# Queries loaded and paired outputs stored in 4096-byte pieces per partition

## The chip, the cores and the metric

The kernel runs on one core of a Trainium2 chip. A core has a matrix engine (TensorE, called PE in the profile; its weight loads are shown apart as PEld), a vector engine (VectorE, DVE), an engine for activation functions (ScalarE, ACT), a general engine (GpSimd, POOL), and an engine that mostly issues transfers (SyncE, SP; its queue is SPq). Sixteen DMA engines move data between the device memory and the on-chip memory of 128 partitions. The engines run side by side, each through its own list of instructions in order; semaphores hold one back until another has come far enough.

The metric is the device time of one execution in microseconds (us); lower is better.

## The reference

The kernel computes an attention over spatially reduced keys, then a mixture of eight small adapters of which each token uses the best two. Reduced to what matters (4 batches of 12288 tokens of 128 channels; 768 pooled keys for a batch):

```python
kv_pool = kv.reshape(B, H // 4, 4, W // 4, 4, C).mean(axis=(2, 4))
k = v = kv_pool.reshape(B, -1, C) @ w_sr
a = softmax(q @ k.T / sqrt(C))
x = a @ v                                   # 49152 tokens x 128
logits = x @ w_gate                         # 8 gates; the best 2 are kept
w = softmax(best 2 logits)
out = x + sum over the 2 chosen e of w[e] * ((x @ A[e]) @ B[e])
```

Every token is computed by itself, given the keys and values of its batch. So the order in which tokens are put into partitions does not matter for the result, as long as the outputs are stored where the queries came from.

## The kernel before, in words

**Tiles.** A chunk is 512 tokens: 128 partitions times four tokens (`NS = 4`). There are 96 chunks (`NCH`), 24 to a batch. Two neighbouring chunks, 2i and 2i + 1, form a pair of 1024 tokens (`HROWS`). Queries are loaded by pairs, gates are sent by pairs, outputs are mostly stored by pairs.

**Which token sits where.** `load_q` (L100) reads a pair as `(k p s) c -> p k (s c)`: partition p holds, of each chunk k of the pair, the four neighbouring tokens 4p to 4p + 3. These are 4 x 128 x 4 bytes = 2048 bytes side by side in device memory, once for each of the two chunks, 256 KB apart. Two more places load queries in the same order: L125 loads the first four chunks (`q0`, 1 MB) in one transfer, and `load_half` (L127) the pairs 2 and 3 into buffers that later hold kv rows. The outputs follow: `give` (L510) gathers a pair in one tile `osb` and stores it in one transfer of the same form (L518), `put` (L503) stores the single chunks at the end of the program, 2048 bytes from each partition, 256 KB in one stretch of the device memory.

**Way of a chunk.** The queries of a pair are cast to 16 bits (`cast_q`, POOL, L107) and turned by a DMA transpose (`turn_q`, SPq, L117), so that channels lie across partitions. `scores` (L326, L327) multiplies keys with them on PE, two key tiles of 128 at a time, and takes the exponential on ACT. `weigh` (L338) multiplies the exponentials with the values; `normalise` (L345 to L356) divides by the sum and finds the best gates on DVE. `gate` (POOL, L365 to L369) and a tanh on ACT make the gates of a pair. They are turned by a small DVE transpose, written to device memory (`send_gates`, L425 and L426) and read back, broadcast over the rows of the adapters (`load_gates`, L433, tile `ge`). The output of `normalise` is turned on PE (L405) and copied by DVE (L416), multiplied with A (L440), gated by DVE (L443, which needs `ge`), multiplied with B (L486) and added to x (L500).

**Order.** It is written out by hand. The main loop (L683) runs over the chunks; in one turn it issues the scores of a later chunk, the weighing of the chunk before, and the adapter stages of chunks six to nine turns back (`lag`, L668). In every second turn it also issues the transpose of the queries three pairs ahead, the load of the queries about five pairs ahead, and the transfers of the gates. The kv rows of the next batch are loaded (L87) and summed (POOL, L191 to L196) in turns fixed by `plan` (L276). Nearly every transfer is issued by SPq, one after another, in this order. Only the four small weight loads at the start are issued by ACT.

**Start.** SPq issues the four kv rows of the first key tile, then `q0`, then the eight kv rows of tiles 1 and 2, then four query loads of 512 KB. The first four chunks are turned on PE (L590) and not by DMA. The last six chunks have their own code after the loop (from L749), in which single chunks are stored by `put`.

Of the kernel before, what the change touches and what calls it, by code (L numbers as in the profile page):

```python
# [21 lines left out]
def kernel(  # L22
# [10 lines left out]
    nc = tc.nc  # L33
    P = 128
# [6 lines left out]
    NTOK = 512  # L41
    NS = NTOK // P
# [31 lines left out]
    qflat = q.rearrange("b n c -> (b n) c")  # L74
# [14 lines left out]
    def load_kv(b, t):  # L89
        for d in range(4):  # L90
            load_row(b, t, d)

    GROWS = 2048

    HROWS = GROWS // 2
    q32, q16, qT = {}, {}, {}

    def load_q(i):  # L100
        q32[i] = qpool.tile([P, 2, NS * C], FP32, tag="q32", name="q32", bufs=3)
        nc.sync.dma_start(q32[i], qflat[i * HROWS:(i + 1) * HROWS].rearrange(
            "(k p s) c -> p k (s c)", p=P, s=NS))

    def cast_q(i):
        new_q16(i)
# [13 lines left out]
    q0, q1 = q01[:, 0], q01[:, 1]  # L120
    for t in range(NT):
        load_kv(0, t)
        if t == 0:

            nc.sync.dma_start(q0, qflat[0:GROWS].rearrange("(k p s) c -> p k s c", p=P, s=NS))  # L125

    def load_half(i):  # L127
        q32[i] = q1[:, 2 * i - 4:2 * i - 2].rearrange("p k s c -> p k (s c)")
        nc.sync.dma_start(q32[i], qflat[i * HROWS:(i + 1) * HROWS].rearrange(
            "(k p s) c -> p k (s c)", p=P, s=NS))  # L130

    load_half(2)
    load_q(4)
    load_half(3)
    load_q(5)

    w_in = const.tile([P, P], FP32)
# [359 lines left out]
    def add_rows(c, lo=0, hi=NS, osb=None, bank_=None):  # L497
        osb = half_out() if osb is None else osb
        d = dps[c][:, lo:hi] if bank_ is None else bank_
        nc.vector.tensor_tensor(osb[:, lo:hi], d, xn[c][:, lo:hi, 0:C], op=ALU.add)  # L500
        return osb

    def put(c, osb, lo=0, hi=NS, queue=None):  # L503
        t0 = c * NTOK
        (queue or nc.sync).dma_start(
            out[t0:t0 + NTOK, :].rearrange("(p s) c -> p s c", p=P)[:, lo:hi], osb[:, lo:hi])

    opair = {}

    def give(c):  # L510

        if c % 2 == 0:
            opair[c // 2] = run.tile([P, 2, NS, P], FP32, tag="osb", name="osb", bufs=3)
        o = opair[c // 2]
        add_rows(c, osb=o[:, c % 2])
        if c % 2:
            t0 = (c - 1) * NTOK
            nc.sync.dma_start(  # L518
                out[t0:t0 + 2 * NTOK, :].rearrange("(k p s) c -> p k (s c)", p=P, k=2),
                o.rearrange("p k s c -> p k (s c)"))  # L520

    spare = []

# [159 lines left out]
    for c in range(2, NCH - 1):  # L683
        b, k = divmod(c, CPB)
# [4 lines left out]
        if c % 2 and (c + 11) // 2 < 2 * NQ:  # L689
            load_q((c + 11) // 2)  # L690
# [12 lines left out]
        for x in ups.get(c, ()):  # L703
            up(x, None if x == ups[c][-1] else t_bank())
            give(x)
# [103 lines left out]
    n = NCH - 1  # L809
# [22 lines left out]
    gated_hidden(n - 6)  # L832
    up(n - 7, bank(0))
    put(n - 7, add_rows(n - 7))
    weigh(n - 1, 1)
    tops4(n - 1, top4, y4)
# [33 lines left out]
    turn(high(n), 0, NS, bank(0), xT, n)  # L870
    add(n - 6, o6, nc.gpsimd)
    put(n - 6, o6)
    gate_args(n, 0, NS, nc.gpsimd, top5, arg5, msk5)
    gate_tanh(0, NS, arg5)
    up(n - 3, mtile([P, NTOK], name="d2"))
    gated(n - 1, 0, NS, arg4, h4)
    put(n - 3, add_rows(n - 3))
    up(n - 2)
    o3 = take(n - 2)
# [33 lines left out]
    with tc.If(bad_v != 0):  # L913
# [11 lines left out]
        with tc.For_i(0, B) as b:  # L925
            nc.sync.dma_start(kp, kp_all[bass.ds(b, 1)].rearrange("o p k -> p (o k)"))
            for h in range(2):
                s = slice(h * NKV // 2, (h + 1) * NKV // 2)
# [3 lines left out]
            for h in range(2):  # L932
                v_ps = mtile([P, NJ // 2, C + E], name="gv_ps")
                for g in range(NJ // 2):
                    j = h * NJ // 2 + g
# [3 lines left out]
            with tc.For_i(0, N, P) as t:  # L939
                t0 = b * N + t  # L940
# [19 lines left out]
                for h in range(2):  # L960
                    e_ps = mtile([P, NJ // 2, P], name="ge_ps")
                    for g in range(NJ // 2):
                        j = h * NJ // 2 + g
# [70 lines left out]
```

## Time and profile before

| | |
|---|---|
| median of 3 runs | 376.8 us (375.92 to 378.57) |
| the profiled execution, its time | 375.43 us |
| the profiled execution, its span from first to last instruction | 373.6 us |
| instructions | 10589 |
| DMA packets, bytes | 95594, 101.01 MB |
| read from device memory, written to it | 62.33 MB, 25.90 MB |
| mean granted clock of TensorE | 0.996 |

The span begins with the first instruction and ends with the last; the execution's own time holds some 1.8 us more. In a row of grouped instructions stand the line of the kernel, the engine, the operation, what is written and read, the count, the busy time in all and the mean time of one. In a timeline the first two columns are the start and the length in us, and a bracket gives the idle time before and what ended it. In a list of waits the columns are the time in all, how often, and the longest. Transfers are cut into packets, one for each piece that is contiguous on both sides; the DMA share is the time of the packets over the time of 16 engines, and since packets of one engine can overlap, it can be above 1.

### The profile page before, as it was taken

The page shows a single profiled execution, that of the slowest core. Times are in us where ns is not written, and L with a number is a line of the kernel's source. Part 1 is how long each engine was busy: PE and PEld are TensorE (multiplying, and loading weights), DVE is VectorE, ACT ScalarE, POOL GpSimd, SP SyncE. Part 2 cuts the span into 40 slices and gives each one's busy share as a digit, 9 for nine tenths or more (in the row PEclk, how much of TensorE's full clock was granted, in tenths as well). Part 3 has the DMA queues.
Part 4 walks back from the last instruction along what each step waited for, and adds up shares of the span by engine and source line. Part 5 has one row for each costly group of instructions (what it writes and reads, how often), then busy time and mean ns, then how long its engine had stood idle before and what let it go on. Part 6 is the DMA issues. An engine that isn't in the chain of part 4 may idle for free.

```text
span 373.6 us, 10589 instructions
## 1 busy us (share of the span) xinstructions
PE 356.5 (95%) x3942; PEld 262.8 (70%) x3943; DVE 299.6 (80%) x952; ACT 309.4 (83%) x391; POOL 225.6 (60%) x376
## 2 busy tenths in 40 slices
PE   4789999999999999999999999999999999999983
PEld 2456777777777677777777777777776767667772
DVE  3784558888888788888888888888888898998983
ACT  1579999989889798898898898898888888888862
POOL 1013799988799897755679697755444234232255
PEclk9999999999999999999999999999999999999998
DMA  8998999999999999999999999998789799663325
GB/s 261 413 360 218 316 300 304 298 318 306 286 335 320 308 292 331 226 317 314 304 288 361 303 313 317 253 302 260 227 225 257 206 255 245 184 145 131 130 86 201
DMA packets 95594, 101.01 MB, mean 270 GB/s; under 512 B 58804, under 2 KB 59060, under 8 KB 95540
## 3 DMA queue, kind: packets, MB, share of 16 engines
q1 hardware_dynamic: 94068, 100.11, 94.6%
q8 instruction: 31, 0.51, 0.6%
q10 hardware_dynamic: 1472, 0.20, 0.3%
q14 instruction: 23, 0.19, 0.2%
HBM read 62.33 MB, written 25.90 MB: 236 GB/s over the span
## 4 chain that ended last, share of the span: by engine, by line
PE 83%; DVE 5%; POOL 4%; DMA 3%; ACT 2%; issue 1%; SPq 0%; POOLq 0%; DVEq 0%
PE xps L338 33%; PE sg L326 30%; PE t_ps L405 5%; PE d_ps L486 5%; PE h_ps L440 4%; DMA kvt<-in_kv_dram 2%; DMA ge<-g_h 2%; ACT tt L327 1%; PE v_ps L215 1%; POOL osb L495 1%; DVE xn_all L349 1%; DVE osb L500 1%; DVE ht L443 1%; DVE kvt L191 1%; PE k_ps L240 1%
## 5 line engine op out<-in xcount | busy, mean ns | idle before, releaser
L327 ACT ACTIVATE tt<-sg 128x1024 f16<-128x1024 f32 x288 | 276.9, 1023 | 36.3 <-PE sg L326 35.5
L326 PE MATMUL sg<-qT,kfT 128*128 128x512 f16 x576 | 170.2, 379 | 0.5 <-ACT qT L593 0.3
L338 PEld LDWEIGHTS <-tt 128*128 128x128 f16 x2304 | 146.1, 98 | 28.4 <-DVE xn_all L349 18.1
L338 PE MATMUL xps<-vext,tt 128*128 128x136 f16 x2256 | 164.7, 223 | 0.3 <-DVE xn_all L349 0.2
L500 DVE TENSOR_TENSOR osb<-d_ps,xn_all 128x512 f32<-128x512 f32 x85 | 58.7, 691 | 28.7 <-PE d_ps L486 27.7
L365 POOL TENSOR_TENSOR arg<-xn_all,top 128x64 f32<-128x64 f32 x47 | 14.5, 308 | 99.6 <-DVE top L356 80.2
L349 DVE TENSOR_TENSOR xn_all<-xps,rinv_all 128x540 f32<-128x540 f32 x94 | 67.7, 721 | 3.3
L326 PEld LDWEIGHTS <-kfT 128*128 128x128 f16 x576 | 49.1, 98 | 24.4 <-issue 1.5
L191 POOL TENSOR_TENSOR kvt<-kvt 128x1024 f32<-128x1024 f32 x27 | 63.7, 2361 | 2.1 <-PE t_ps L405 2.0
L107 POOL CAST q<-q 128x1024 f16<-128x1024 f32 x45 | 46.8, 1042 | 24.0 <-DMA q<-in_q_dram 24.0
L443 DVE SCALAR_TENSOR_TENSOR ht<-ge,h_ps 128x512 bf16<-128x512 f16 x87 | 58.5, 673 | 1.4 <-DMA ge<-g_h 1.0
L486 PEld LDWEIGHTS <-ht 128*128 128x128 bf16 x368 | 27.0, 98 | 24.6 <-DVE ht L443 5.7
L356 DVE MAX8 top<-xn_all 128x8 f32<-128x8 f32 x376 | 35.1, 156 | 6.3
L416 DVE COPY xt<-t_ps 128x512 bf16<-128x512 bf16 x92 | 36.8, 400 | 0.0
L405 PE MATMUL t_ps<-id_bf,xn_all 128*128 128x128 bf16 x376 | 36.3, 219 | 0.0
L486 PE MATMUL d_ps<-b_bf,ht 128*128 128x128 bf16 x340 | 32.9, 219 | 0.8 <-DVE ht L443 0.7
L440 PE MATMUL h_ps<-xt,a_bf 128*128 128x512 bf16 x86 | 32.6, 379 | 0.1
L345 DVE RECIPROCAL rinv_all<-xps 128x4 f32<-128x4 f32 x94 | 17.1, 182 | 13.6 <-PE xps L338 12.2
L405 PEld LDWEIGHTS <-xn_all 128*128 128x128 bf16 x376 | 25.9, 98 | 0.3
L368 POOL TENSOR_SCALAR msk<-msk 128x64 f32<-128x64 f32 x47 | 20.2, 429 | 4.1
L369 POOL TENSOR_TENSOR arg<-arg,msk 128x64 f32<-128x64 f32 x47 | 15.1, 321 | 3.9
L367 POOL TENSOR_TENSOR arg<-arg,msk 128x64 f32<-128x64 f32 x47 | 15.1, 320 | 3.7
(150 smaller groups left out, 221.0 us busy)
## 6 DMA issues: line engine op xcount, KB each, us to landing
kvt<-in_kv_dram SPq DMA_DIRECT2D x48, 512.0 KB
q<-in_q_dram SPq DMA_DIRECT2D x46, 512.0 KB
out_dram<-osb SPq DMA_DIRECT2D x44, 512.0 KB
ge<-g_h SPq DMA_DIRECT2D x45, 256.0 KB
out_dram<-osb SPq DMA_DIRECT2D x8, 256.0 KB
q<-in_q_dram SPq DMA_DIRECT2D x1, 1024.0 KB
qT<-q SPq DMA_TRANSPOSE x46
g_h<-g_sb SPq DMA_DIRECT2D x45, 16.0 KB
```

The source lines that it names most:

```text
L107: nc.gpsimd.tensor_copy(q16[i], q32[i].rearrange("p k n -> p (k n)"))
L191: eng.tensor_tensor(v[:, 0], v[:, 0], v[:, d], op=ALU.add)
L326: mm(sg[:, k], kfT[b][:, j * P:(j + 1) * P], qc, start=True, stop=True)
L327: nc.scalar.activation(tt[c][:, 2 * r:2 * r + 2], sg, AF.Exp, bias=0.0, scale=scale)
L338: mm(o, tt[c][:, j, s * P:(s + 1) * P], vext[b][:, j, 0:VW], start=(j == 0 and s % 2 == 0), stop=(j == NJ - 1 and s % 2 == 1), skip_group_ ...
L349: nc.vector.tensor_tensor(xn[c][:, :, 0:C + G].rearrange("p (b s) v -> p b s v", b=2), xv[:, :, :, 0:C + G], ri.rearrange("p (b s) -> p b ...
L405: mm(columns(t_ps, c, s), src[:, s], id_bf, is_transpose=True, start=(s == 0), stop=(s == NS - 1), skip_group_check=True)
L416: nc.vector.tensor_copy(to, t_ps)
L440: mm(h_ps, a_bf, xT[c], start=True, stop=True)
L443: nc.vector.scalar_tensor_tensor(hgT[c].rearrange("p (k a) t -> p k (a t)", k=2), gE[c // 2][:, h:h + NS // 2].rearrange("p a t k -> p k ( ...
L486: mm(dps[c][:, s], columns(hgT[c], c, s), b_bf, start=(s == 0 and fresh), stop=(s == NS - 1), skip_group_check=True)
L500: nc.vector.tensor_tensor(osb[:, lo:hi], d, xn[c][:, lo:hi, 0:C], op=ALU.add)
```

## The change

Partition p holds eight neighbouring tokens of a pair, 8p to 8p + 7: the first four count as its tokens of the even chunk, the last four as those of the odd chunk. Query loads (L100, L125, L127) and paired stores (`give`) then have one piece of 4096 bytes for each partition and pair, where they had two of 2048. `put`, which stores a single chunk, writes 2048 bytes from each partition into every other 2048 bytes of the pair's place. Nothing else is changed: tiles, buffers and the order of all instructions are as before.

```diff
@@ load_q
-        nc.sync.dma_start(q32[i], qflat[i * HROWS:(i + 1) * HROWS].rearrange(
-            "(k p s) c -> p k (s c)", p=P, s=NS))
+        nc.sync.dma_start(q32[i].rearrange("p k n -> p (k n)"), qflat[
+            i * HROWS:(i + 1) * HROWS].rearrange("(p t) c -> p (t c)", p=P))
@@ the first four chunks
-            nc.sync.dma_start(q0, qflat[0:GROWS].rearrange("(k p s) c -> p k s c", p=P, s=NS))
+            nc.sync.dma_start(
+                q0.rearrange("p (j k) s c -> p j (k s c)", k=2),
+                qflat[0:GROWS].rearrange("(j p t) c -> p j (t c)", p=P, j=2))
@@ load_half
-        nc.sync.dma_start(q32[i], qflat[i * HROWS:(i + 1) * HROWS].rearrange(
-            "(k p s) c -> p k (s c)", p=P, s=NS))
+        nc.sync.dma_start(q32[i].rearrange("p k n -> p (k n)"), qflat[
+            i * HROWS:(i + 1) * HROWS].rearrange("(p t) c -> p (t c)", p=P))
@@ put
-        t0 = c * NTOK
+        t0 = c // 2 * HROWS
         (queue or nc.sync).dma_start(
-            out[t0:t0 + NTOK, :].rearrange("(p s) c -> p s c", p=P)[:, lo:hi], osb[:, lo:hi])
+            out[t0:t0 + HROWS, :].rearrange("(p k s) c -> p k s c", p=P, k=2)[:, c % 2, lo:hi],
+            osb[:, lo:hi])
@@ give
-                out[t0:t0 + 2 * NTOK, :].rearrange("(k p s) c -> p k (s c)", p=P, k=2),
-                o.rearrange("p k s c -> p k (s c)"))
+                out[t0:t0 + HROWS, :].rearrange("(p t) c -> p (t c)", p=P),
+                o.rearrange("p k s c -> p (k s c)"))
```

## The prediction

> **What bounds the kernel now.** I read the page's first two parts, then the stages (busy time by window), TensorE's timeline inside a stage, the waits, and at last the DMA side that the change touches. The page first: busy time by engine, then tenths in 40 slices.
>
> ```profile
> PE 356.5 (95%) x3942; PEld 262.8 (70%) x3943; DVE 299.6 (80%) x952; ACT 309.4 (83%) x391; POOL 225.6 (60%) x376
> PE   4789999999999999999999999999999999999983
> PEclk9999999999999999999999999999999999999998
> DMA  8998999999999999999999999998789799663325
> DMA packets 95594, 101.01 MB, mean 270 GB/s; under 512 B 58804, under 2 KB 59060, under 8 KB 95540
> q1 hardware_dynamic: 94068, 100.11, 94.6%
> ```
>
> Two resources look full: TensorE (PE, 95%) and the 16 DMA engines (94.6% of their time, nearly all on one queue). Which one sets the end? The stages answer that; their columns are busy us (x instructions) of PE, weight loads, DVE, ACT, POOL, then granted clock, DMA share and GB/s.
>
> ```profile
> 0.00:30.00 30.00, 21.54 (x115) 11.89 (x116) 18.62 (x33) 15.00 (x21) 3.90 (x13) 1.00 0.89 328
> 30.00:120.00 90.00, 89.78 (x1016) 66.80 (x1015) 67.67 (x237) 81.70 (x102) 74.92 (x106) 1.00 1.10 302
> 120.00:130.00 10.00, 9.27 (x108) 7.12 (x107) 7.71 (x23) 8.19 (x12) 8.74 (x11) 1.00 1.10 325
> 130.00:270.00 140.00, 140.00 (x1595) 105.51 (x1594) 118.89 (x388) 123.92 (x157) 99.39 (x153) 1.00 1.09 295
> 270.00:300.00 30.00, 29.85 (x337) 21.66 (x334) 26.16 (x81) 25.38 (x30) 10.51 (x24) 1.00 0.86 223
> 300.00:350.00 50.00, 49.95 (x567) 36.33 (x567) 44.98 (x151) 42.99 (x52) 16.52 (x41) 1.00 0.68 192
> 350.00:373.60 23.60, 16.16 (x217) 13.46 (x214) 15.53 (x45) 12.20 (x23) 11.63 (x30) 0.94 0.37 132
> ```
>
> From 30 to 350 us PE is busy 318.85 of 320: 0.22 idle, then 0.73, then 0.00, 0.15 and 0.05, in all 1.15 us. The DMA share falls there from 1.10 to 0.68 (above 1 because packets on one engine overlap), and PE does not get faster when it falls: so PE is the bound. That its busy time is real work shows in its timeline, where the period of one 512-token chunk is constant:
>
> ```profile
> 102.15 0.87 PE L338 MATMUL xps<-vext,tt 128*128 128x136 f16 x12
> 105.53 0.87 PE L338 MATMUL xps<-vext,tt 128*128 128x136 f16 x12
> 108.91 0.87 PE L338 MATMUL xps<-vext,tt 128*128 128x136 f16 x12
> 128.05 0.40 PE L486 MATMUL d_ps<-b_bf,ht 128*128 128x128 bf16 x4 [0.73 <-DVE ht L443]
> ```
>
> 3.38 us each time, 6.75 for the pair of chunks that shares one query load and one output store. The last line is the one visible stall: 0.73 us, behind DVE's L443, which itself waited for a DMA. The first and last 30 us are the only others with idle PE (8.46 and 7.44 us).
>
> **The change part by part.** Both programs have the same instructions in the same order, with the same waits, on all five engines; only the access patterns of 47 query loads, 44 paired stores and 8 single stores differ. So no compute term changes. The DMA terms: the page's list of issues and, for the time that SyncE's queue (SPq) spends issuing, the rows of the tiles (min/median/max ns).
>
> ```profile
> q<-in_q_dram SPq DMA_DIRECT2D x46, 512.0 KB
> out_dram<-osb SPq DMA_DIRECT2D x44, 512.0 KB
> out_dram<-osb SPq DMA_DIRECT2D x8, 256.0 KB
> q<-in_q_dram SPq DMA_DIRECT2D x1, 1024.0 KB
> L102 SPq DMA_DIRECT2D q<-in_q_dram x44: 368/582/1225, 15.7 to 313.4; - x44
> L87 SPq DMA_DIRECT2D kvt<-in_kv_dram x48: 534/580/1366, 0.7 to 221.4; - x48
> L117 SPq DMA_TRANSPOSE qT<-q x46: 1265/1962/4162, 27.8 to 333.7; - x46
> ```
>
> *Issue.* A query load of today has 256 pieces of 2048 bytes, a kv row 128 pieces of 4096, both 512 KB: medians 582 and 580 ns. Issuing costs the same in either form: 0.
>
> *Moving.* The stages in which one kind of piece has the DMA engines to itself give its rate: kv rows (4096) from 13 to 20.5 us, query loads (2048) from 22.2 to 26, single output stores (2048) at the end.
>
> ```profile
> 13.00:20.50 7.50, 6.57 (x39) 3.92 (x37) 5.46 (x8) 6.89 (x11) 0.00 (x0) 1.00 1.03 419
> 22.20:26.00 3.80, 3.48 (x26) 2.20 (x25) 3.17 (x6) 2.42 (x5) 0.00 (x0) 1.00 1.05 406
> 369.00:373.60 4.60, 0.27 (x2) 0.09 (x2) 0.41 (x2) 0.00 (x0) 0.31 (x1) 0.69 0.50 189
> ```
>
> Per full share that is 419/1.03 = 407, 406/1.05 = 387 and 189/0.50 = 378 GB/s. A pair of chunks loads 0.524 MB and stores 0.524 MB: 1.049 MB take 2.71 us at 387 and 2.58 at 407, so 0.13 us of DMA time is saved per pair. A store in pieces of 4096 bytes is not in this trace; I take the kv rows' 407 for it too, since loads and stores in 2048 are near each other (387, 378), and keep 10% dearer than today as the bad end (a rival below). Hidden behind it: PE's 6.75 us. Saved DMA time is not saved time unless something waits on DMA. Who does?
>
> ```profile
> DVE kvt L191 <- DMA kvt<-in_kv_dram: 3.0, 2, 1.8
> POOL q L107 <- DMA q<-in_q_dram: 24.0, 1, 24.0
> DVE ht L443 <- DMA ge<-g_h: 1.0, 1, 1.0
> ```
>
> *Start, DVE's wait for kv (3.0 us).* The 1 MB of first queries goes ahead of kv tiles 1 and 2, so their rows land 1.049/387 - 1.049/407 = 0.13 us sooner. DVE's sums then end sooner, but PE is not ready for them:
>
> ```profile
> 19.61 0.42 DVE L196 TENSOR_TENSOR kvt<-kvt 128x256 f32<-128x256 f32 x1
> 24.60 0.43 DVE L196 TENSOR_TENSOR kvt<-kvt 128x256 f32<-128x256 f32 x1
> 19.11 1.46 PE L605 MATMUL w_ps<-id_bf 128*128 128x512 bf16 x6
> 24.18 1.07 PE L338 MATMUL xps<-vext,tt 128*128 128x136 f16 x12
> 27.11 0.64 DVE L615 CAST q<-q 128x512 f16<-128x512 f32 x1
> ```
>
> Tile 1 is summed at 20.03, PE is in line ahead of it until 20.57; tile 2 at 25.03, PE until 25.25. Gain 0; at most 0.13. *POOL's 24 us* is its wait for the first cast. The four 512 KB loads before it (2.1 MB) land up to 0.27 us sooner, but the first transpose is issued at 27.8 (the L117 row above), when DVE's own cast of a query tile ends (27.11 + 0.64), and from 30 us on PE has next to no gap. Gain 0; at most 0.27.
>
> *Middle, the gate broadcast (1.0 us of DVE, 0.73 of PE).* SPq's own timeline before it:
>
> ```profile
> 114.18 0.58 SPq L102 DMA_DIRECT2D q<-in_q_dram  x1
> 114.86 0.41 SPq L518 DMA_DIRECT2D out_dram<-osb  x1
> 116.69 4.13 SPq L117 DMA_TRANSPOSE qT<-q  x1
> 120.92 0.59 SPq L426 DMA_DIRECT2D g_h<-g_sb  x1
> 121.56 0.80 SPq L433 DMA_DIRECT2D ge<-g_h  x1
> ```
>
> The transpose kept SPq for 4.13 us, against 1.27 at best, after a query load and a store had been queued; the two gate transfers stood behind it. The shorter transfers ahead save 0.13 us for this pair, and more if the backlog of earlier pairs shrinks as well. Ends: 0 (and then something near 0.7 stays) and -0.73; I take the middle, -0.4. The saved time is not lost elsewhere: PE next waits for nothing.
>
> *Tail.* The eight single stores keep 2048-byte pieces, now every 4096 bytes in DRAM. Nothing waits for them but the end. The last three, 0.79 MB, take 2.1 us at 378 GB/s; no row shows such a stride in a store. Ends: 0 and +2.1 (half the rate). I take 0: the piece, and so the packet, is the same.
>
> Sum: 0 + 0 - 0.4 + 0 = -0.4 us. The profiled execution took 375.43 us, its span 373.6 and 1.8 around it, so 375.0 for it. That run lies 1.4 under the median of 376.8; against the median the forecast is 376.4.
>
> **The rivals.** *DMA is the real bound after all* (faster). For it: a share of 1.10 over 90 us. Then each pair would save 0.13 us; between 30 and 240 us, where kv loads run too, are 210/6.75 = 31 pairs, so 4.0 us: 372.8. Against it: 140.00 busy us of 140 on PE, and the same period where DMA has room. The Trainium skill, "DMA: Bandwidth & Descriptors", section "Why small descriptors are slow (HBM only)", gives a fixed cost of about 3 cycles per packet beside one cycle per 32 bytes; by that two packets of 2048 take 134 cycles and one of 4096 takes 131, 2.2% less. With it the saving would be an estimated 0.06 us per pair and this rival only 1.9 us, 374.9. The rows here show 5% (387 to 407), so I go by the rows.
>
> *4096-byte stores are dear and DMA becomes the bound* (slower). The place is the stretch from 30 to 240 us, where the share is 1.09 to 1.10 already, and the gate broadcast stands in SPq behind the transpose. If query and output pieces cost 10% more than today, a pair takes 0.27 us longer on the DMA engines; with no room left, 31 pairs make 8.4 us: 385.2. It decides over 1% (3.8 us) from 0.12 us per pair, 4.5% dearer, if there is no room at all. For it: one late broadcast already. Against it: 4096-byte kv rows are the fastest transfers of the trace.
>
> *The strided single stores are slow* (a little slower): 2.1 us, 378.5, as worked out above.
>
> *The change does less than said*: the pieces stay 2048 bytes because a transfer is cut up anyway. Then the time is 376.8. Against it: the kv rows do move in 4096-byte pieces, at a rate that the 2048-byte loads don't reach.
>
> **How the numbers follow.** A difference under 1% (3.8 us) is what a measurement of this kernel can't well tell from none. Forecast (376.4) 0.74; pieces not changed or of no effect (376.8) 0.06; slow tail (378.5) 0.07; dear pieces (385.2, or less) 0.09; DMA the bound (372.8) 0.04. The first three lie within 1%: 0.87; slower 0.09; faster 0.04. Range: below, 376.8 less the whole stall (0.73), less the start's 0.13 + 0.27, less the 0.9 by which the fastest of the three runs (375.92) lies under the median: 374.8. Above, the slow tail, 378.5, and the slowest of the runs (378.57): 378.6. Out of it stay the two outer rivals, 0.13.
>
> **What would show it.** Packets should fall by 46 x 128 + 256 for the queries and 44 x 128 for the stores, 11776: from 95594 to 83818. The stage of pure query loads near 25 us should move about 419 GB/s. PE's chunk period must stay at 3.38 us, the wait of L443 for the gate broadcast should shrink or go, and the last stage keep its 23.6 us. A longer period, many waits of L443 for DMA, or transposes that hold SPq longer than their median of 1962 ns would prove the forecast wrong in the direction of the slower rival; PE idle in the middle of the span would show where.

## The result, and the profile after

| | before | changed |
|---|---|---|
| median of the 11 runs that stood side by side | 376.37 us (375.55 to 380.62) | 378.75 us (377.39 to 380.91) |
| ratio to the kernel before, 95% interval | | 1.0063 (1.004 to 1.0087) |
| profiled execution: time, span | 375.43, 373.6 us | 380.12, 378.3 us |
| DMA packets | 95594 | 83818 |

The changed kernel is 0.6% slower. The forecast of 376.4 was in effect no change (0.4 us less than before), and its range ended at 378.6. The profiled execution lies 1.4 us above the median of the changed kernel, so what it shows is one of its worse cases. The page of the changed kernel, in the parts that stand above for the kernel before:

```profile
PE 359.5 (95%) x3943; PEld 264.2 (70%) x3943; DVE 299.5 (79%) x952; ACT 309.5 (82%) x391; POOL 225.4 (60%) x376
PE   3859999999999999999999999999999999999983
PEclk9978999999999999999999999999999999999998
DMA  7895999999999999999999999997778798754425
DMA packets 83818, 101.01 MB, mean 267 GB/s; under 512 B 58804, under 2 KB 59060, under 8 KB 83764
q1 hardware_dynamic: 82292, 100.11, 91.7%
```

The packets fell by 11776, exactly as counted, and the queue's share from 94.6% to 91.7%. What is new stands in the third and fourth slice (19 to 38 us): less PE in the third, a lower granted clock in both, DMA engines at half load in the fourth. The same by stages (PE, weight loads, DVE, ACT, POOL, clock, DMA share, GB/s; the rows from 270 to 300 us and from 350 us on are left out):

```profile
0.00:30.00 30.00, 19.26 (x78) 9.94 (x79) 16.48 (x27) 10.53 (x17) 1.97 (x12) 0.90 0.88 320
30.00:120.00 90.00, 89.57 (x994) 66.12 (x992) 64.79 (x224) 81.49 (x100) 71.40 (x102) 1.00 1.05 291
120.00:130.00 10.00, 10.00 (x116) 7.50 (x114) 8.49 (x30) 8.95 (x13) 9.59 (x12) 1.00 1.11 301
130.00:270.00 140.00, 140.00 (x1598) 105.84 (x1596) 119.14 (x386) 123.90 (x157) 100.16 (x153) 1.00 1.07 297
300.00:350.00 50.00, 49.87 (x561) 35.91 (x560) 44.69 (x147) 42.30 (x52) 17.08 (x41) 1.00 0.72 192
```

From 120 to 270 us TensorE has no gap in this execution; the stall of 0.73 us for the gate broadcast is missing, and in the list of waits L446 (the old L443) waits for no DMA. (Whether the change did that is a question for the last runs.) The first 30 us did 78 matmuls where the kernel before did 115. So the loss must lie in the start. TensorE's timeline there, first the kernel before, then the changed one:

```profile
20.40 0.38 PE L232 MATMUL kp_ps<-id_f,kvt 128*128 128x128 f32 x2
21.26 0.70 PE L240 MATMUL k_ps<-kp_keep,w_sr_sb 128*128 128x256 f32 x2 [0.47 <-ACT kp_keep L235]
30.87 0.88 PE L338 MATMUL xps<-vext,tt 128*128 128x136 f16 x12 [0.17 <-DVE xn_all L349]
```

```profile
23.45 0.46 PE L235 MATMUL kp_ps<-id_f,kvt 128*128 128x128 f32 x2 [2.88 <-DVE kvt L199]
24.39 1.22 PE L243 MATMUL k_ps<-kp_keep,w_sr_sb 128*128 128x256 f32 x2 [0.47 <-ACT kp_keep L238]
36.46 0.88 PE L341 MATMUL xps<-vext,tt 128*128 128x136 f16 x12 [0.17 <-DVE xn_all L352]
```

The same three steps come 3.05, 3.13 and 5.59 us later. Two things add up: TensorE stands idle for 2.88 us before kv tile 1, and then it is slow (the second step takes 1.22 us instead of 0.70). Of the 5.59 us, 0.9 are won back later, 0.73 of them in the missing stall: the span is 4.7 longer. The slowness is the clock:

```profile
22.00:24.00 2.00, 0.46 (x2) 0.20 (x2) 1.90 (x4) 0.05 (x1) 0.00 (x0) 0.94 1.03 420
24.00:26.00 2.00, 1.22 (x2) 0.65 (x3) 1.89 (x3) 0.69 (x2) 0.00 (x0) 0.50 1.02 416
28.00:30.00 2.00, 2.00 (x11) 1.37 (x11) 0.41 (x1) 1.56 (x3) 0.29 (x1) 0.50 0.84 344
32.00:34.00 2.00, 1.91 (x11) 0.98 (x10) 0.83 (x4) 1.81 (x3) 0.00 (x0) 1.00 0.00 0
```

The granted clock falls to 0.50 right after the gap and is back at 1.00 by 32 us. The Trainium skill, "TensorE: Matmul & The Clock Gate", Part 1, says that an idle window of about 3.4 us puts the engine at half its clock; the trace agrees on the half, and here a gap of 2.88 us with little work around it was enough.

Why was kv tile 1 late? SyncE's queue had stopped. Its waits in the first 30 us, before and after (total, times, longest):

```profile
SPq L87 <- DMA a_f<-in_moe_A_dram: 4.6, 1, 4.6
SPq L87 <- DMA b_f<-in_moe_B_dram: 0.4, 1, 0.4
```

```profile
SPq L87 <- DMA a_f<-in_moe_A_dram: 7.0, 1, 7.0
SPq L87 <- DMA b_f<-in_moe_B_dram: 0.9, 1, 0.9
```

L87 loads kv rows and needs nothing of a_f or b_f, the adapter weights that ACT's queue loads. But in the trace's instruction records the transfers issued from SP and ACT take turns on eight completion semaphores (numbers 100 and 102 to 108). The third kv row of tile 1 gets number 104, which a_f has, and the fourth gets 105, which b_f has; so they can't be issued before the weights have landed. While SyncE waits, its transfers run out (first the kernel before, then the changed one):

```profile
14.00:16.00 2.00, 2.00 (x16) 1.52 (x15) 0.89 (x1) 1.64 (x4) 0.00 (x0) 1.00 1.03 418
```

```profile
14.00:16.00 2.00, 2.00 (x15) 1.50 (x14) 0.97 (x4) 1.64 (x4) 0.00 (x0) 1.00 0.48 87
```

That this wait ends in TensorE's gap is read from the chain of work that ended last in the first 30 us of the changed kernel (start, length, what):

```profile
2.20 13.02 DMA b_f<-in_moe_B_dram
15.24 5.66 DMA kvt<-in_kv_dram
20.99 1.24 DVE kvt L194
23.45 0.47 PE kp_ps L235 x2
```

b_f, which stands behind a_f on ACT's queue, lands at 15.22 us. The fourth kv row of tile 1 is issued at 15.24 and lands at 20.90, then DVE sums it. DVE has waited for the weights itself (1.2 us for a_f, 1.0 for b_f), but after that it stands idle twice more for kv rows (1.08 and 1.82 us): the rows come last.

And why did a_f land later? It consists of 1024 pieces of 64 bytes. In the packet records of the traces some of the last of them start at these times (us). The records name the queue and not the engine; starts so evenly spaced are read here as those of one engine:

```
query pieces of 1024 bytes (run e9)   9.918   9.967  10.017  10.066    every  49 ns
query pieces of 2048 (before)         9.527   9.614   9.701   9.788    every  87 ns
query pieces of 4096 (changed)       12.156  12.319  12.481  12.643    every 162 ns
query pieces of 8192 (run e3)        10.323  10.636  10.949  11.262    every 313 ns
```

A piece of 2048 bytes takes 84 ns, one of 4096 takes 159 (medians of the same records), each 3 ns less than the spacing. So an engine that has work from both queues moves one piece of the one, then one of the other, and each small piece waits that long for its turn. Half of the a_f packets are through by 5.9 us in both kernels; a rest is left when the 1 MB of queries arrives, and the last a_f packet starts at 10.40 us before, at 13.10 after. The Trainium skill, "DMA: Bandwidth & Descriptors", section "Queues, rings and completion order", says that an engine serves its queues in turn, a packet at a time, and that a packet is typically some 9 to 17 descriptors. The trace agrees on the turns and not on their length: with these transfers a turn was one piece, whatever its size.

### The profile page after: what moved, and what is told of

It reads as the page before. It is cut to its first block, busy times and chain, and to the rows that moved or that the text cites. A ratio compares the mean times of both kernels' runs of the same rounds, so it can differ in the third digit from the quotient of the medians.

```text
span 378.3 us, 10590 instructions
## 1 busy us (share of the span) xinstructions
PE 359.5 (95%) x3943; PEld 264.2 (70%) x3943; DVE 299.5 (79%) x952; ACT 309.5 (82%) x391; POOL 225.4 (60%) x376
## 2 busy tenths in 40 slices
DMA packets 83818, 101.01 MB, mean 267 GB/s; under 512 B 58804, under 2 KB 59060, under 8 KB 83764
## 3 DMA queue, kind: packets, MB, share of 16 engines
q1 hardware_dynamic: 82292, 100.11, 91.7%
## 4 chain that ended last, share of the span: by engine, by line
PE 83%; DMA 5%; DVE 4%; POOL 4%; ACT 1%; issue 1%; ACTq 0%; POOLq 0%; DVEq 0%
PE xps L341 34%; PE sg L329 30%; PE t_ps L408 5%; PE d_ps L489 5%; PE h_ps L443 5%; DMA b_f<-in_moe_B_dram 3%; DMA kvt<-in_kv_dram 1%; PE v_ps L218 1%; POOL osb L498 1%; ACT tt L330 1%; DVE xn_all L352 1%; PE kp_ps L210 1%; POOL q L108 1%; DVE osb L503 1%; PE k_ps L243 1%
## 5 line engine op out<-in xcount | busy, mean ns | idle before, releaser
L446 DVE SCALAR_TENSOR_TENSOR ht<-ge,h_ps 128x512 bf16<-128x512 f16 x87 | 58.5, 672 | 0.5
L443 PE MATMUL h_ps<-xt,a_bf 128*128 128x512 bf16 x87 | 33.0, 379 | 0.1
```

Of the source, the lines that this page charges most:

```text
L443: mm(h_ps, a_bf, xT[c], start=True, stop=True)
L446: nc.vector.scalar_tensor_tensor(hgT[c].rearrange("p (k a) t -> p k (a t)", k=2), gE[c // 2][:, h:h + NS // 2].rearrange("p a t k -> p k ( ...
```

## The experiments

Theory A: the loss arises only at the start, where the larger query pieces hold up the small weights on ACT's queue, these hold up SyncE, and TensorE goes idle and loses clock. Theory B: 4096-byte pieces cost something in every pair. Theory C: the clock differs by itself, whatever the loads do. Each ratio is to the kernel before, timed on the same chip; all line numbers are those of the run's own kernel.

**e1: the changed kernel, with the first four chunks as before.**

```diff
-            nc.sync.dma_start(
-                q0.rearrange("p (j k) s c -> p j (k s c)", k=2),
-                qflat[0:GROWS].rearrange("(j p t) c -> p j (t c)", p=P, j=2))
+            nc.sync.dma_start(q0, qflat[0:GROWS].rearrange("(k p s) c -> p k s c", p=P, s=NS))
...
+            if c < 4:
+                nc.sync.dma_start(
+                    out[t0:t0 + 2 * NTOK, :].rearrange("(k p s) c -> p k (s c)", p=P, k=2),
+                    o.rearrange("p k s c -> p k (s c)"))
...
```

> The changed kernel with the first four chunks as before: their 1 MB query load in 2048-byte pieces, the stores of pairs 0 and 1 to match; all other query loads and paired stores stay in 4096-byte pieces. Theory A (start): the loss arises only where the 1 MB load shares the DMA engines with the small adapter weights that ACT's queue loads; larger pieces make those weights land later, SyncE cannot issue the next kv rows until they have landed, TensorE goes idle and its clock then drops. So this kernel is at or a little under the kernel before, 375.5 to 376.6 us, the wait of SyncE for a_f is near 4.6 us and the first stage as in the kernel before. Theory B (steady state): 4096-byte loads and stores cost time in every pair; then it stays near 378.5. Theory C (clock alone, not the loads): the time stays spread between 377.4 and 381.

Measured: 375.87 us, ratio 0.9987 (0.9968 to 1.0006). The loss is gone with 1 MB of 25 MB of queries; SyncE waits 4.9 us for a_f.

**e2: the kernel before, with only the first four chunks changed** (the same edit the other way).

> The kernel before with only the first four chunks changed: their 1 MB query load in 4096-byte pieces, the stores of pairs 0 and 1 to match; everything else in 2048-byte pieces. Theory A: the whole loss is here, 378 to 379.5 us, SyncE's wait for a_f near 7 us, TensorE idle for some 2.9 us before it turns key tile 1. Theory B: at most one pair's share of the loss, 376.3 to 376.6. Theory C: no prediction of a difference between this kernel and the one before.

Measured: 378.91 us, 1.0078 (1.0052 to 1.0104). One load and two stores make the whole loss. Its profiled execution has the same picture:

```profile
SPq L87 <- DMA a_f<-in_moe_A_dram: 6.8, 1, 6.8
23.42 0.44 PE L234 MATMUL kp_ps<-id_f,kvt 128*128 128x128 f32 x2 [2.52 <-DVE kvt L198]
26.00:28.00 2.00, 2.00 (x8) 1.34 (x7) 1.93 (x3) 0.69 (x1) 0.00 (x0) 0.50 1.05 406
```

Theory B is out, since e1 keeps the larger pieces in all other pairs and has no loss. C is out too: the same load moves the time in both directions.

**e3: the first four chunks in pieces of 8192 bytes**, the stores of pairs 0 and 1 to match.

```diff
             nc.sync.dma_start(
...
+                q0.rearrange("p k s c -> p (k s c)"),
+                qflat[0:GROWS].rearrange("(p t) c -> p (t c)", p=P))
```

> The changed kernel with the first four chunks as one group: partition p holds 16 neighbouring tokens, so that the 1 MB query load has one piece of 8192 bytes for each partition. If the pieces move whole, theory A says that the small weights land later still: SyncE's wait for a_f about 7.0 + 2.4 = 9.4 us or more, and the time 380 to 384 us. If a piece of 8192 bytes is cut into packets of 4096, theory A says the same as for the changed kernel, 378 to 379.5. Theory B: 378.5, since the steady state is that of the changed kernel.

Measured: 379.77 us, 1.0093 (1.0068 to 1.0119), with SyncE's wait at 6.8 us. The pieces do move whole:

```profile
DMA packets 83690, 101.01 MB, mean 267 GB/s; under 512 B 58804, under 2 KB 59060, under 8 KB 83508
```

182 packets are not under 8 KB, 128 more than in the changed kernel (54). So I was wrong on the size: a piece twice as long did not add the expected 2.4 us to the wait, although each turn took 313 ns. The load has then only 8 pieces for each engine. After them come the few kv rows that were queued already, in pieces of 4096, and when they are through, the small pieces share with nobody; that this caps the wait is argued from the records, not shown by a run.

**e4: the weights on SyncE's queue, ahead of the 1 MB load.**

```diff
+            nc.sync.dma_start(a_f, moe_A.rearrange("e c r -> c e r"))
+            nc.sync.dma_start(b_f, moe_B.rearrange("e r c -> r e c"))
             nc.sync.dma_start(
                 q0.rearrange("p (j k) s c -> p j (k s c)", k=2),
...
-    nc.scalar.dma_start(a_f, moe_A.rearrange("e c r -> c e r"))
...
-    nc.scalar.dma_start(b_f, moe_B.rearrange("e r c -> r e c"))
```

> The changed kernel with the two adapter weight loads (a_f, b_f) issued by SyncE between the kv rows of tile 0 and the 1 MB query load, instead of by ACT: they then stand in the same queue and share turns with nothing. Theory A: a_f has landed by about 10 us, SyncE does not wait for it, the start is no later than in the kernel before, 375.3 to 376.6 us; TensorE shows no gap over 1 us before key tile 1. Theory B: near 378.5, since the steady state is untouched. Theory C: spread between 377.4 and 381.

Measured: 376.21 us, 0.9996 (0.997 to 1.0022), with all 4096-byte pieces in place. SyncE does not wait for a_f or b_f, and TensorE has no gap over 0.7 us at tile 1.

**e11: the weights on GpSimd's queue, all else as in the changed kernel** (`nc.gpsimd.dma_start` for `nc.scalar.dma_start`). This was meant to part the late landing from SyncE's wait.

> The changed kernel with a_f and b_f loaded through GpSimd's queue instead of ACT's, at the same point of the program; DVE's copies stay where they were. SyncE's kv rows then no longer wait for a_f or b_f (they share no completion semaphore with them), while the small pieces still share the DMA engines with the 4096-byte pieces and may land as late as before. If SyncE's wait is the link: 375.3 to 376.8, no wait of SyncE for a_f, TensorE without the gap ahead of key tile 1. If late weights hurt by themselves (DVE waits for them ahead of tile 1): 377.5 to 379.5.

Measured: 375.82 us, 0.9991 (0.9974 to 1.0008), and no wait of SyncE for a_f or b_f. But the weights did not land late on this way: a_f lands 7.2 us after its issue at 1.3 us, b_f 6.9 us after 2.4, and the records show them as 32 packets of 4096 bytes instead of small pieces. So this run, like e4, takes away the late landing and SyncE's wait together, and the time is back; it does not part the two. The next run does more for that.

**e7: the DVE copies of the weights moved behind the sums of kv tile 1** (`if t == 0` becomes `if t == 1`).

> The changed kernel with the three DVE copies that need the adapter weights moved from behind the sums of kv tile 0 to behind those of tile 1; the weights are still loaded by ACT's queue. It takes the one use of the late weights out of the way of tile 1 and leaves SyncE's wait in place. If the loss comes from SyncE, which can't issue the kv rows of tile 1 while it waits for a_f and b_f: no gain, 377.8 to 379.5, and SyncE's wait for a_f stays near 7 us where a_f lands late. If it came from DVE standing in line behind the late weights: back to 375.5 to 376.6.

Measured: 377.8 us, 1.0045 (1.0018 to 1.0072), 375.07 to 379.95 over 12 runs: still slower than before, by 1.96 us of median. DVE can no longer hold tile 1 up for the weights here, and most of the loss stays: so SyncE's wait is the link, and the chain above says the same. In its profiled execution, a quick one of 376.39 us, a_f happened to land early:

```profile
SPq L87 <- DMA a_f<-in_moe_A_dram: 4.2, 1, 4.2
21.29 0.70 PE L243 MATMUL k_ps<-kp_keep,w_sr_sb 128*128 128x256 f32 x2 [0.47 <-ACT kp_keep L238]
```

With the wait at 4.2 us there is no such gap and no low clock, though the pieces are 4096 bytes. So the larger pieces don't delay a_f in each execution. The profiled executions with the weights on ACT's queue say more. The column in the middle counts those of the 1024 a_f packets that still start after 8.6 us, about when the 1 MB of queries arrives:

| pieces of the 1 MB | a_f packets after 8.6 us | third kv row of tile 1 is issued at |
|---|---|---|
| 2048 bytes: before, e1 | 91, 148 | 10.96, 11.57 us |
| 4096: e5, e7, e14, e2, changed | 9, 15, 46, 118, 122 | 9.90, 10.81, 12.42, 13.39, 13.79 us |

With little left, a_f is early whatever the pieces; with a rest left, it is late with the larger pieces, and already with 46 packets later than with 148 beside the smaller ones. That would also be why the runs of the changed kernel spread. Whether the moved copies are worth part of the 0.95 us between the medians (377.8 and 378.75) is open: the intervals overlap.

**e5: more filler matmuls in the gap** (`warm(6)` becomes `warm(18)`).

> The changed kernel with 18 instead of 6 filler matmuls on TensorE before key tile 1, about 2.6 us more of them; the kernel has them only to keep the engine busy, and their result is not used. They lie in the 2.9 us in which the changed kernel's TensorE waits for that tile. Theory A with the clock as a second step: the wait for the kv rows stays (about 23 us until tile 1 is turned), but the granted clock does not fall to 0.5 from 24 to 30 us, and the time falls by about 1 us against the changed kernel, to 377 to 378, less spread. If the lower clock were not caused by the idle gap, it stays low and the time stays at 378.5 or above.

Measured: 377.44 us (376.82 to 378.27), 1.0027 (1.0004 to 1.005). The mean clock was 0.995 or more in all 12 runs; in the changed kernel it was 0.990 or less in 7 of 11 (the drop from 23.74 to 30.57 us of its profiled execution takes 0.009 off the mean). Those 7 runs have a median of 378.81, the other 4 one of 377.6, so the low clock, with whatever longer gap goes with it, is worth about 1.2 us, and e5 lies where the runs without it lie. Such a clock is seen in 6 of 10 runs of e2, in none of the 49 of e1, e4, e8 and e11, and in 4 of the 86 runs of the kernel before that stood beside the experiments (378.31 to 378.95 us): the kernel before has the same weakness, only seldom. The profiled execution of e5:

```profile
SPq L87 <- DMA a_f<-in_moe_A_dram: 3.5, 1, 3.5
19.30 4.05 PE L609 MATMUL w_ps<-id_bf 128*128 128x512 bf16 x18
24.04 0.70 PE L243 MATMUL k_ps<-kp_keep,w_sr_sb 128*128 128x256 f32 x2 [0.47 <-ACT kp_keep L238]
```

The step is at full speed (0.70), but a_f landed early in this execution, so it does not show the fillers in a gap; that they keep the clock up rests on the 12 runs. It does show their price: DVE has summed tile 1 at 19.67 us, and the fillers keep TensorE until 23.2, needed or not.

**e9: the kernel before, with the first four chunks in pieces of 1024 bytes** (`"(m p t) c -> p m (t c)"` with t = 2).

> The kernel before with the first four chunks in 1024-byte pieces (two neighbouring tokens of a partition), queries and the stores of pairs 0 and 1. Theory A: the adapter weights get a turn after each piece and so land sooner than before (last a_f packet near 9.5 us against 10.4), SyncE's wait for a_f falls from 4.6 to 3.5 to 4.2 us; the time gains little, since in the kernel before TensorE is in line ahead of key tile 1 anyway: 375.4 to 376.6. If the size of the pieces had nothing to do with that wait, it stays at 4.6.

Measured: 375.91 us, 0.9991 (0.9971 to 1.0012); SyncE's wait 2.9 us, the last a_f packet at 10.13. The wait is 1.7 us shorter than before, but mostly because it began later: the first kv row of tile 1 took 1.8 us to issue behind the 1 MB in 1024-byte pieces. It ended at 10.57 us, against 10.96. So a_f landed little sooner, and a single execution can't tell this from chance. The time gains nothing, as expected, since in the kernel before TensorE is busy ahead of tile 1 until 20.57 us anyway.

**e8 and e10: the weights last, for the changed kernel and for the one before.** Both issue a_f and b_f on SyncE behind the query loads of the start, and use them after the first chunk's normalisation.

```diff
-    nc.scalar.dma_start(a_f, moe_A.rearrange("e c r -> c e r"))
+    nc.sync.dma_start(a_f, moe_A.rearrange("e c r -> c e r"))
...
-        if t == 0:
-            nc.vector.tensor_copy(a_bf.rearrange("p (r e) -> p e r", e=E),
...
     normalise(0)
+    nc.vector.tensor_copy(a_bf.rearrange("p (r e) -> p e r", e=E),
```

> The changed kernel with the two adapter weight loads issued by SyncE after the query loads of the start, and the three DVE copies that use them moved behind the first chunk's normalisation (they are needed only some chunks later). Nothing small then shares the DMA engines with the 1 MB query load and the first kv rows but w_in and w_gate. Theory A: no wait of SyncE for a_f or b_f, first stage no later than in the kernel before, 374.8 to 376.3 us. Theory B: 378.5.

> The kernel before with the same edit as in the run with late weights: adapter weights after the query loads of the start, on SyncE. Beside that run it tells what 4096-byte pieces are worth once the start does not depend on them. Theory A with a TensorE-bound middle: the two are alike within 0.5 us, both 374.8 to 376.3. If larger pieces were a gain in the middle, this one is over 1 us slower than the other; if they were a loss there (theory B), over 1 us faster.

Measured: e8 374.81 us, 0.9964 (0.9942 to 0.9985), a little faster than the kernel before and well under the changed one; e10 375.63, 0.9988 (0.9967 to 1.0009). They differ by 0.8 us, not by under 0.5, though the intervals overlap. From 120 to 270 us, e8 first and then e10:

```profile
120.00:270.00 150.00, 150.00 (x1716) 113.44 (x1713) 127.46 (x411) 133.11 (x169) 108.38 (x165) 1.00 1.07 294
```

```profile
120.00:270.00 150.00, 149.40 (x1703) 112.64 (x1701) 126.91 (x410) 132.40 (x168) 108.55 (x165) 1.00 1.09 297
DVE ht L443 <- DMA ge<-g_h: 0.9, 1, 0.9
```

It looks as if the larger pieces had removed the stall of the middle. But e1, e4, e7 and e11 have those pieces there too, and the stall. So four kernels were profiled once more.

**e12, e13, e14, e15: e8, e11, the changed kernel and e10 once more**, unchanged, one profiled execution each (375.52, 374.81, 377.53 and 375.69 us).

> The kernel of the run with late weights once more, for one more profiled execution. Question: does TensorE's stall behind the gate broadcast near 127 us belong to the size of the pieces, to the kernel, or to the single execution? If to 4096-byte pieces (none) or to the kernel: no stall between 40 and 345 us again. If to the execution: it can be there, 0.5 to 1.1 us.

> The kernel with the weights on GpSimd's queue once more; its first profiled execution had a stall of 1.0 us there although all its pieces in the middle have 4096 bytes. If the stall belongs to the kernel, it is there again, near 1.0; if to the execution, it can be missing.

> The changed kernel once more; its first profiled execution had no stall there. If it belongs to the kernel: none again. If to the execution: it can be there. At the start, theory A: SyncE's wait for a_f anywhere between 3.5 and 7 us, and TensorE's gap ahead of tile 1 only where that wait is over about 5.

> The kernel before with late weights once more; it had a stall of 0.6 us there, as all four profiled executions with 2048-byte pieces in the middle. If 2048-byte pieces bring it: there again. If it is a matter of the execution: it can be missing.

Measured: the first three changed sides. e12 has the stall that e8 lacked, e13 has not the one of e11, e14 has one where the first execution had none; e15 has it as before. TensorE's waits between 40 and 350 us in e12 and e14:

```profile
PE d_ps L489 <- DVE ht L446: 1.1, 1, 1.1
```

```profile
PE d_ps L489 <- DVE ht L446: 0.6, 1, 0.6
```

So with 4096-byte pieces it is a matter of the execution: 6 of 11 profiled executions have it (0.6 to 1.1 us, e1 0.8, e4 1.1, e7, e11 1.0), a mean of 0.5 over the eleven; with 2048-byte pieces 5 of 5 have it (before, e2, e9, e10, e15; 0.5 to 0.8), a mean of 0.64. A gain in the middle of over some tenths is not shown. Why e8 is faster than e10 stays open; the second chunk is weighed from 31.00 and 30.57 us on in the profiled executions of e8 and e12, and from 31.10 and 31.27 in those of e10 and e15.

e14 adds a case between to the start:

```profile
SPq L87 <- DMA a_f<-in_moe_A_dram: 6.4, 1, 6.4
22.24 0.44 PE L235 MATMUL kp_ps<-id_f,kvt 128*128 128x128 f32 x2 [1.76 <-DVE kvt L199]
23.15 0.70 PE L243 MATMUL k_ps<-kp_keep,w_sr_sb 128*128 128x256 f32 x2 [0.47 <-ACT kp_keep L238]
33.06 0.89 PE L341 MATMUL xps<-vext,tt 128*128 128x136 f16 x12 [0.17 <-DVE xn_all L352]
```

A wait of 6.4 us, a gap of 1.76, and no drop of the clock: 377.53, where the first execution (7.0, 2.88, clock down) took 380.12. The three steps come 1.84, 1.89 and 2.19 us later than before: without the drop the delay hardly grows, where with it it grew from 3.13 to 5.59.

## Why the prediction was wrong

- *What bounds the kernel:* right. TensorE is the bound from 30 to 350 us, and from 120 to 350 us it has no more idle time than before. The reading behind it was too narrow: the period of a chunk is not constant. From 130 to 152 us of the kernel before it runs from 3.38 to 3.89 us; only the busy time is the same (140.00 of 140 us in both).
- *Issue and count:* right on the count (83818). A query load and a kv row were thought to cost the same to issue, and the median of the query loads stayed (582 ns before, 581 after). The paired stores got cheaper to issue, which was not foreseen (last section).
- *The start, DVE's wait for kv:* this step failed. It said that the 1 MB load ahead of kv tiles 1 and 2 would let their rows land 0.13 us sooner, "Gain 0; at most 0.13", and set no bound for a loss. It looked at the one queue and its bytes. The waits of SyncE's queue were not used, and they held the warning: 4.6 us of L87 for a_f, a transfer of another queue, while tile 1 had only 0.54 us to spare (summed at 20.03, TensorE ready at 20.57). In the profiled execution the rows came 3 us later, and the low clock took 2.5 more; over the runs it makes 2.4 us of median. e1 and e2 show the place, the chain and e7 the link; e4, e8 and e11 take it away.
- *The middle:* right that nothing else happens there and that the stall can go, but it does not go reliably. The term of -0.4 was mis-sized: 0.5 us on average against 0.64 is -0.1, within the scatter of so few executions.
- *The tail:* right, 0. From the first single store to the end it is 373.6 - 358.8 = 14.8 us before and 378.3 - 363.5 = 14.8 after, by the rows of the stores (before, then after):

```profile
L505 SPq DMA_DIRECT2D out_dram<-osb x8: 332/357/805, 358.8 to 369.3; - x8
L508 SPq DMA_DIRECT2D out_dram<-osb x8: 332/333/383, 363.5 to 374.0; - x8
```

- *The rivals:* none of them was it. The slower one put the price into every pair (30 to 240 us) and into the cost of the piece itself; the pieces move at their old price (159 ns for 4096 bytes, against twice 84), and who pays is a small transfer that takes turns with them. One sign that was to speak for the slower rival came all the same: the transposes hold SPq for a median of 2197 ns, against 1962. It cost nothing there, since TensorE has no gap from 120 to 270 us. Only the price of a packet was weighed, and not the turns of two queues.
- *The sum:* for -0.4 it should have read about +2.4, all of it start. The range had the tail as its upper end, at 378.6; the median lies 0.15 above it. That differences under 1% can't be told from none was too careful: eleven runs of each kernel tell 0.6%.

## What to carry to other kernels

A larger piece was not only cheaper for its own transfer (159 ns for 4096 bytes, against twice 84), it was a longer turn for the other queue on the same engines (162 ns, against 87). Before enlarging pieces, look for small transfers that run at the same time on another queue, and for who waits until they have landed, be it only through a shared completion semaphore. Small loads that are needed late can be issued late (e8), or on the same queue ahead of the large ones (e4).

## What was not expected of the hardware

The DMA engines alternated piece by piece between two queues, from 1024 to 8192 bytes (49, 87, 162 and 313 ns between two small pieces). Gaps of 2.23 us (e3), 2.52 (e2) and 2.88 (changed kernel) on TensorE were enough to halve its granted clock for 3.4 to 6.8 us; one of 1.76 us (e14) was not. A paired store of one piece for each partition was issued in a median of 372 ns, where the store of two pieces took 626. No gain in the time is seen from it:

```profile
L518 SPq DMA_DIRECT2D out_dram<-osb x44: 372/626/2040, 62.2 to 355.1; - x44
```

```profile
L522 SPq DMA_DIRECT2D out_dram<-osb x44: 332/372/1287, 67.8 to 359.8; - x44
```

Left open: why the number of small pieces that are left when the 1 MB load comes differs so much between executions (9 to 148).
